# Attention's second product on 128 partitions instead of 99: probabilities padded with rows of zeros, values with rows of ones

## The chip, the cores and the metric

The kernel runs on one core of a Trainium2 chip. The metric is the device time of one execution in microseconds (us). Before the change it is 1243.13 us, the median of three runs (1242.87 to 1243.32).

Engines in the profile: PE is TensorE's matmul, PEld its weight load, DVE is VectorE, ACT is ScalarE, POOL is GpSimd, SP is the engine that issues most transfers. A matmul here has a stationary operand (loaded by a weight load, contraction rows x 128 columns) and a moving operand (the same contraction rows x N columns). N is called the width below, and the number of contraction rows is called the rows.

## The reference, cut to what matters

Two independent parts are put side by side along the last axis. Part A is a state-space layer. Part B, which the change touches, is attention over 64 segments of 32 tokens, each with 8 memory tokens, 32 heads of 128:

```python
for s in range(n_seg):                                   # 64 segments
    h = concat([mem, x[:, s*32:(s+1)*32]], axis=1)       # 40 rows
    q, k, v = h @ Wq, h @ Wk, h @ Wv                     # 32 heads of 128
    p = softmax(where(mask, q @ k.T * 128**-0.5, -1e9))
    o = (p @ v) @ Wo                                     # p @ v is the "second product"
    mem = o[:, :8]
    outs.append(o[:, 8:])
```

## The kernel before

It guesses the memory rows first, so that all segments can be worked on at once, and checks the guess at the end. Three segments and their three memory rows make one block of GW = 99 keys (96 tokens, GX = 96, and 3 memory rows). A unit is two heads by two blocks: four first products (k by q), one Exp on ACT, one masking product on POOL, and four second products. There are 16 head pairs x 11 units = 176 units, so 704 second products.

```python
# qk_init: buffers of the second product
for i in range(2):
    t = pool.tile([GW, NG, VW], BF16, name=f"b_v{i}", bufs=1)    # values: 99 partitions, 22 blocks, VW = 258
    G.memset(t[:, :, 0:1], 1.0)                                   # a column of ones gives the softmax sum
    G.memset(t[:, :, VW - 1:VW], 1.0)
for i in range(4):
    t = pool.tile([GW, 4 * GW + 32], BF16, name=f"b_m{i}", bufs=1)  # masked probabilities
    G.memset(t[:, 4 * GW:4 * GW + 32], 0.0)

def att_front(self, hp, u):
    for gg in range(2):
        g0 = (2 * u + gg) * GW
        for hh in range(2):
            j = 2 * gg + hh
            PE.matmul(s[:, j * GW:(j + 1) * GW], kt[:, hh, g0:g0 + 128], qt[:, hh, g0:g0 + GW], start=True, stop=True)
    # ... e = exp(s) on ACT ...
    k.G.tensor_tensor(v4(m[:, 0:4 * GW]), v4(e[:]), mask..., ALU.mult)   # POOL
    return m

def att_back(self, hp, u, m):
    for gg in range(2):
        for hh in range(2):
            j = 2 * gg + hh
            cs = slice(hh * 129, hh * 129 + 129)                  # 128 values and the ones column
            PE.matmul(o[:, gg, cs], m[:, j * GW:j * GW + 128], vt[:, 2 * u + gg, cs], start=True, stop=True)
    # ... reciprocal of the sums and normalisation on DVE ...

def attention(self):                                              # cut
    for n, (hp, u) in enumerate(units):
        pend.append((hp, u, self.att_front(hp, u)))
        if len(pend) > 2:
            self.att_back(*pend.pop(0))
        yield hp, u                                               # the projections of the next head pair go in between
```

So a unit is four matmuls of 99 columns on 128 rows, then four of 129 columns on 99 rows. What follows a unit has 128 rows again: a projection of 480 columns after 142 of the 176 units, and matmuls of 201, 512 or 73 columns after the other 34.

Of the kernel before, what the change touches and what calls it, by code (L numbers as in the profile page):

```python
# [9 lines left out]
BF16 = mybir.dt.bfloat16  # L10
I32 = mybir.dt.int32
ACT = mybir.ActivationFunctionType
ALU = mybir.AluOpType
# [17 lines left out]
NG = 22; GX = 96; GW = 99; NU = NG // 2  # L31
# [9 lines left out]
VW = 258  # L41
# [275 lines left out]
class PartB:  # L317
# [201 lines left out]
    def qk_init(self, pool):  # L519
        V, G = self.k.V, self.k.G  # L520
        self.qk = []
        for i in range(2):
            pair = []
            for n in "qk":
                t = pool.tile([128, 2, QW], BF16, name=f"b_{n}{i}", bufs=1)
                V.memset(t[:, :, 64 + NMX:GX], 0.0)
                V.memset(t[:, :, 21 * GW + 64:21 * GW + GX], 0.0)
                V.memset(t[:, :, NG * GW:QW], 0.0)
                pair.append(t)
            self.qk.append(pair)  # L530
        self.vmst = []
        for i in range(2):
            t = pool.tile([128, 4, 128], BF16, name=f"b_vmst{i}", bufs=1)
            V.memset(t[:, :, NM:128], 0.0)
            self.vmst.append(t)
        self.vb, self.mb = [], []
        for i in range(2):
            t = pool.tile([GW, NG, VW], BF16, name=f"b_v{i}", bufs=1)
            G.memset(t[:, :, 0:1], 1.0)
            G.memset(t[:, :, VW - 1:VW], 1.0)  # L540
            self.vb.append(t)
        for i in range(4):
            t = pool.tile([GW, 4 * GW + 32], BF16, name=f"b_m{i}", bufs=1)
            G.memset(t[:, 4 * GW:4 * GW + 32], 0.0)
            self.mb.append(t)

# [56 lines left out]
    def att_front(self, hp, u):  # L603
        k = self.k; PE = k.PE
        qt, kt = self.qk[hp % 2]
        s = k.ps("S")
# [5 lines that stand above are left out]
        e = self.p3.tile([GW, 4 * GW], BF16, name="b_e", bufs=3)  # L612
        i = hp * NU + u
        k.S.activation(e[:], s[0:GW, 0:4 * GW], ACT.Exp, scale=float(E) ** -0.5, accum_out=self.accE[0:GW, i:i + 1])  # L614
        m = self.mb[i % 4]
        mask = k.maskA if u == 0 else k.maskB
        v4 = lambda t: t.rearrange("p (a b q) -> p a b q", a=2, b=2)
        k.G.tensor_tensor(v4(m[:, 0:4 * GW]), v4(e[:]), mask[0:GW, :, :].unsqueeze(2).to_broadcast([GW, 2, 2, GW]), ALU.mult)  # L618
        return m

    def att_back(self, hp, u, m):
# [515 lines left out]
```

## Time and profile before

| what | number | where |
|---|---|---|
| span of the profiled run | 1240.8 us | head of the page |
| PE busy | 1234.9 us (100%) | busy table |
| PE waiting | 2.2 us, all in the first 16 us | list of waits |
| second product, first to last matmul | 502.0 to 1017.1 us | instructions of the values' tile |
| POOL idle before its first mask product | 31.15 us | timeline of POOL |

From the page of the kernel before: its head, two rows of its slices (PE, and the clock granted to it) and its chain by engine. In the slices each digit is for 1/40 of the span, in tenths:

```profile
span 1240.8 us, 19711 instructions
PE 1234.9 (100%) x8148; PEld 655.2 (53%) x8148; DVE 611.2 (49%) x1124; ACT 325.9 (26%) x754; POOL 199.9 (16%) x284
PE   9999999999999999999999999999999999999998
PEclk9999999999999999999999999999999999999999
PE 98%; DMA 1%; DVE 0%; issue 0%
```

The last of these lines is the chain of waits that ended last, by engine. PE is the limit from the first slice to the last, and the granted clock is 1.0 in the run's record. Apart from the 2.2 us of waits, nothing can shorten the run but a shorter matmul stream.

The list of waits of PE, before (who waited for whom, total us, times, longest us):

```profile
PE psO L913 <- PEq L1118: 0.9, 1, 0.9
PE psO L379 <- DMA a_hs<-in_B_x_dram: 0.6, 1, 0.6
PE psS L414 <- DVE b_xe L77: 0.5, 1, 0.5
PE psS L414 <- DMA a_hs<-in_B_Wv_dram: 0.2, 1, 0.2
```

The groups by shape, before (line, engine, operation, output<-inputs, output shape<-input shape, count, busy us, mean ns of one, idle before):

```profile
L629 PE MATMUL psO<-b_v,b_m 99*128 99x129 bf16 x704 | 70.4, 221 | 0.0
L611 PE MATMUL psS<-b_q,b_k 128*128 128x99 bf16 x704 | 60.1, 208 | 0.0
L629 PEld LDWEIGHTS <-b_m 99*128 99x128 bf16 x704 | 46.4, 99 | 0.5
L685 PEld LDWEIGHTS <-b_ol 128*128 128x128 bf16 x960 | 93.1, 98 | 109.3
```

The 221 ns of a second product is its latency; many overlap. What it costs the stream is the time from its start to the start of the next matmul, called its gap here. The weight load of 99 rows takes as long as one of 128.

The trace's records give each matmul's start to the nanosecond. Means by width, before (worked out from the starts):

```
what                          width  rows   gap, ns     width/2.4 + 2.5
output projection                512   128   215.9        215.8
projections                      480   128   202.5        202.5
last tile, third piece           128   128    55.8         55.8
guess                             64   128    29.1         29.2
projections of the memory        201   128    86.7         86.3
first product, 1st..4th of 4      99   128    44.5 44.9 44.0 45.3    43.8
second product, 1st..4th of 4    129    99    60.4 59.3 59.2 59.4    56.3
```

The formula in the last column is from the Trainium skill, "TensorE: Matmul & The Clock Gate", section "Back-to-back issue gap", which gives it for isolated matmuls. The multiples of 32 agree with it here to 0.1 ns, each matmul with its own weight load. The second product is over it by about 3 ns.

These are means over 176 units.

### The profile page before, as it was taken

The page shows a single profiled execution, that of the slowest core. Times are in us where ns is not written, and L with a number is a line of the kernel's source. Part 1 is how long each engine was busy: PE and PEld are TensorE (multiplying, and loading weights), DVE is VectorE, ACT ScalarE, POOL GpSimd, SP SyncE. Part 2 cuts the span into 40 slices and gives each one's busy share as a digit, 9 for nine tenths or more (in the row PEclk, how much of TensorE's full clock was granted, in tenths as well). Part 3 has the DMA queues.
Part 4 walks back from the last instruction along what each step waited for, and adds up shares of the span by engine and source line. Part 5 has one row for each costly group of instructions (what it writes and reads, how often), then busy time and mean ns, then how long its engine had stood idle before and what let it go on. Part 6 is the DMA issues. An engine that isn't in the chain of part 4 may idle for free.

```text
span 1240.8 us, 19711 instructions
## 1 busy us (share of the span) xinstructions
PE 1234.9 (100%) x8148; PEld 655.2 (53%) x8148; DVE 611.2 (49%) x1124; ACT 325.9 (26%) x754; POOL 199.9 (16%) x284
## 2 busy tenths in 40 slices
PE   9999999999999999999999999999999999999998
PEld 4444444444455445566666655655565554454444
DVE  4889999999941222444444444444444550011000
ACT  3344434444310001333333323333333230000000
POOL 2000000000032140222222222232222330000000
PEclk9999999999999999999999999999999999999999
DMA  9942232332566558577668554645575469607000
GB/s 223 260 130 68 85 94 68 102 94 77 153 189 202 158 161 170 100 151 150 138 122 173 123 136 95 129 77 103 106 139 106 72 203 231 140 18 153 17 18 28
DMA packets 306056, 153.95 MB, mean 124 GB/s; under 512 B 147242, under 2 KB 299810, under 8 KB 305962
## 3 DMA queue, kind: packets, MB, share of 16 engines
q1 hardware_dynamic: 304138, 150.82, 52.6%
q10 hardware_dynamic: 1824, 1.84, 0.5%
q8 instruction: 65, 1.06, 0.4%
q14 instruction: 29, 0.24, 0.1%
HBM read 73.70 MB, written 44.71 MB: 95 GB/s over the span
## 4 chain that ended last, share of the span: by engine, by line
PE 98%; DMA 1%; DVE 0%; issue 0%
PE psP L585 33%; PE psS L685 9%; PE psO L256 9%; PE psS L414 9%; PE psP L414 9%; PE psP L685 5%; PE psS L310 4%; PE psP L310 4%; PE psP L568 4%; PE psO L629 3%; PE psS L611 3%; PE psO L685 2%; PE psS L718 1%; PE psP L505 1%; PE psP L737 1%; PE psO L482 1%
## 5 line engine op out<-in xcount | busy, mean ns | idle before, releaser
L585 PE MATMUL psP<-b_xe,w 128*128 128x480 bf16 x2048 | 439.6, 366 | 0.0
L585 PEld LDWEIGHTS <-w 128*128 128x128 bf16 x2048 | 193.7, 98 | 183.5
L618 POOL TENSOR_TENSOR b_m<-b_e,maskB 99x396 bf16<-99x396 bf16 x160 | 139.4, 871 | 348.2 <-ACT b_e L614 348.2
L77 DVE CAST b_q<-psP 128x480 bf16<-128x480 f32 (+1 forms) x192 | 98.1, 532 | 145.4 <-PE psP L585 133.9
L414 PEld LDWEIGHTS <-b_xe 128*128 128x128 bf16 x1024 | 99.8, 98 | 121.3 <-DVE b_xe L77 1.1
L75 ACT ACTIVATE b_k<-psP 128x480 bf16<-128x480 f32 x128 | 73.1, 571 | 319.1 <-PE psP L585 319.1
L685 PEld LDWEIGHTS <-b_ol 128*128 128x128 bf16 x960 | 93.1, 98 | 109.3
L614 ACT ACTIVATE b_e<-psS 99x396 bf16<-99x396 f32 x176 | 87.4, 497 | 170.9 <-PE psS L611 165.5
L636 DVE TENSOR_TENSOR b_ot<-psO,b_rall 99x512 bf16<-99x512 f32 x176 | 121.7, 692 | 6.4
L256 PE MATMUL psO<-w,a_bt 128*128 128x512 bf16 x512 | 115.7, 379 | 0.0
L634 DVE RECIPROCAL b_rall<-psO 99x4 f32<-99x4 f32 x176 | 31.3, 178 | 132.8 <-PE psO L629 132.8
L685 PE MATMUL psS<-w,b_ol 128*128 128x512 bf16 x416 | 92.1, 379 | 0.0
L414 PE MATMUL psS<-w,b_xe 128*128 128x512 bf16 x384 | 90.7, 379 | 0.0
L414 PE MATMUL psP<-w,b_xe 128*128 128x512 bf16 x384 | 90.7, 379 | 0.0
L256 PEld LDWEIGHTS <-a_bt 128*128 128x128 bf16 x512 | 49.7, 98 | 59.0
L310 PEld LDWEIGHTS <-a_hs 128*128 128x128 bf16 x512 | 49.5, 98 | 58.3
L77 DVE CAST b_ost<-psS 128x512 bf16<-128x512 f32 x13 | 9.0, 692 | 125.4 <-PE psS L685 125.4
L629 PE MATMUL psO<-b_v,b_m 99*128 99x129 bf16 x704 | 70.4, 221 | 0.0
L611 PEld LDWEIGHTS <-b_k 128*128 128x128 bf16 x704 | 50.0, 98 | 33.9 <-DVE b_k L77 0.2
L611 PE MATMUL psS<-b_q,b_k 128*128 128x99 bf16 x704 | 60.1, 208 | 0.0
L75 ACT ACTIVATE b_vst<-psS 128x512 bf16<-128x512 f32 x56 | 33.4, 597 | 99.5 <-PE psS L414 75.6
L310 PE MATMUL psS<-w,a_hs 128*128 128x512 bf16 x256 | 57.9, 379 | 0.0
(203 smaller groups left out, 1097.9 us busy)
## 6 DMA issues: line engine op xcount, KB each, us to landing
b_v<-b_vx SPq DMA_DIRECT2D x16, 1056.0 KB
b_os<-b_ot SPq DMA_DIRECT2D x16, 960.0 KB
w<-in_B_Wv_dram SPq DMA_DIRECT2D x14, 1024.0 KB
b_vx<-b_vst SPq DMA_DIRECT2D x48, 256.0 KB
w<-in_B_Wo_dram SPq DMA_DIRECT2D x12, 1024.0 KB
w<-in_B_Wq_dram SPq DMA_DIRECT2D x16, 512.0 KB
w<-in_B_Wk_dram SPq DMA_DIRECT2D x16, 512.0 KB
a_xn<-in_A_x_dram SPq DMA_DIRECT2D x32, 128.0 KB
```

What stands on the lines that cost most here:

```text
L75: self.S.activation(out, in_, ACT.Copy)
L77: self.V.tensor_copy(out, in_)
L256: m = PE.matmul(u[:, i, :], self.bt[:, i, c, :], self.xT[tb][:, c, :], start=(c == 0), stop=(c == KC - 1))
L310: PE.matmul(py[:], self.hs[tb][:, pc, i, tt * 128:(tt + 1) * 128], self.ct[half, i][:, pc, :], start=(pc == 0 and i == 0), stop=(pc == PC ...
L414: m = self.k.PE.matmul(p[:], self.xe[:, c, t * 128:(t + 1) * 128], w[:, c, :], start=(c == 0), stop=(c == KC - 1))
L585: PE.matmul(p[:, 0:480], w[:, i * KC + c, hh * 128:(hh + 1) * 128], self.xe[:, c, 480 * q:480 * q + 480], start=(c == 0), stop=(c == KC - 1))
L611: PE.matmul(s[:, j * GW:(j + 1) * GW], kt[:, hh, g0:g0 + 128], qt[:, hh, g0:g0 + GW], start=True, stop=True)
L614: k.S.activation(e[:], s[0:GW, 0:4 * GW], ACT.Exp, scale=float(E) ** -0.5, accum_out=self.accE[0:GW, i:i + 1])
L618: k.G.tensor_tensor(v4(m[:, 0:4 * GW]), v4(e[:]), mask[0:GW, :, :].unsqueeze(2).to_broadcast([GW, 2, 2, GW]), ALU.mult)
L629: PE.matmul(o[:, gg, cs], m[:, j * GW:j * GW + 128], vt[:, 2 * u + gg, cs], start=True, stop=True)
L636: V.tensor_tensor(ot[:, 2 * u:2 * u + 2, :].rearrange("p g (h e) -> p g h e", h=2), oa[:, :, 1:257].rearrange("p g (h e) -> p g h e", h=2) ...
L685: k.PE.matmul(self.acc[t, half], ol[:, h8, tt * 128:(tt + 1) * 128], self.wo_half(half, h), start=(h == 0), stop=(h == H - 1))
```

## The change

Its intent is to let the second product contract over a full array of 128 rows. Rows 99 to 127 of the probabilities are zero and of the values one, so they add nothing. Exp, the mask product and the normalisation keep 99 partitions. (The mask's index is cut in the last line.)

```diff
-            t = pool.tile([GW, NG, VW], BF16, name=f"b_v{i}", bufs=1)
+            t = pool.tile([128, NG, VW], BF16, name=f"b_v{i}", bufs=1)
+            G.memset(t[GX:128, :, :], 1.0)
             G.memset(t[:, :, 0:1], 1.0)
             G.memset(t[:, :, VW - 1:VW], 1.0)
@@
-            t = pool.tile([GW, 4 * GW + 32], BF16, name=f"b_m{i}", bufs=1)
+            t = pool.tile([128, 4 * GW + 32], BF16, name=f"b_m{i}", bufs=1)
+            G.memset(t[GX:128, :], 0.0)
             G.memset(t[:, 4 * GW:4 * GW + 32], 0.0)
@@ att_front
-        k.G.tensor_tensor(v4(m[:, 0:4 * GW]), v4(e[:]), mask..., ALU.mult)
+        k.G.tensor_tensor(v4(m[0:GW, 0:4 * GW]), v4(e[:]), mask..., ALU.mult)
```

More of the change, by code (lines that the diff above doesn't have):

```diff
@@ L617, in att_front @@
         v4 = lambda t: t.rearrange("p (a b q) -> p a b q", a=2, b=2)
-        k.G.tensor_tensor(v4(m[:, 0:4 * GW]), v4(e[:]), mask[0:GW, :, :].unsqueeze(2).to_broadcast([GW, 2, 2, GW]), ALU.mult)
+        k.G.tensor_tensor(v4(m[0:GW, 0:4 * GW]), v4(e[:]), mask[0:GW, :, :].unsqueeze(2).to_broadcast([GW, 2, 2, GW]), ALU.mult)
         return m
```

## The prediction

> **What bounds the kernel.** TensorE, everywhere. The page's busy table gives PE 1234.9 of 1240.8 us (100%), the chain of waits is 98% PE, and the list of waits shows PE waiting 2.2 us in the whole run, all of it at the start. The granted clock is 1.0 throughout. So time moves only if the matmul stream becomes shorter or gets a hole.
>
> **What the change touches there.** The second attention product: 704 weight loads of b_m (99x128) and 704 matmuls of b_v (99 rows, 129 moving columns), all between 502 and 1017 us. Afterwards they have 128 rows. Nothing is removed and no column is added or taken away.
>
> From the groups by shape: the 99-row weight loads take 98 ns, as do all 128-row loads. The weight loads of both heights have the same four-chunk, 32-column read pattern, so the fast load is already on. The Trainium skill ("TensorE: Matmul & The Clock Gate", section on LDWEIGHTS) says that load time goes with columns, not rows; this trace agrees. The same page ("Back-to-back issue gap") gives N/2.4 + 2.5 ns from start to start. In the timeline of PE, 512 columns take 215.8 ns, 128 take 55.8, 64 take 29.1: exactly that. The second product takes 59.5 ns against 56.25 by the formula, also in the step to the next 128-row matmul (59.4). That is 3.2 ns over, and it doesn't vary with the head's or unit's alignment. Other odd widths with 128 rows are over by less: 73 by 0.8, 99 by 0.8, 201 by 0.4 ns.
>
> So the whole prize is about 3.2 ns x 704 = 2.3 us, 0.2%, if the partial rows cause that excess, and nothing if the odd width of 129 does. I give each about half. There is no larger row penalty hiding: no weight load here delays its matmul, since 64-column matmuls with their own loads run at 29 ns.
>
> **What it adds.** On POOL, at 465.8 us, two fills of 32 partitions x 5676 elements and four of 428. Existing fills took 108 ns for 25, 204 ns for 128 and 258 ns for 198 elements: about 0.85 ns an element, so an estimate of 4.9 us each for b_v and 0.4 us each for b_m, 11.5 us together. POOL is idle from 466.4 to 497.5 us there, and the DMA that first writes b_v is issued at 483.5 us. The fills should be done near 478 us: off the critical path. The per-unit mask product on POOL (871 ns), Exp, reciprocal and eviction keep 99 partitions. SBUF space per partition and DMA are unchanged.
>
> **Prediction.** 1242.0 us, range 1239.8 to 1244.3. Chances: faster by over 2% 0.01, within 2% 0.98, slower by over 2% 0.01.
>
> **What would show it.** Right: PE still busy for 100%; second product's rows 128; its weight loads still 98 ns; the gap from its start to the next start between 56.2 and 59.6 ns (56.2 means rows were the cause, 59.5 the width); POOL busy up by about 11 us, all before 480 us; b_v's DMAs at the same times. Wrong: a PE hole near 480 to 505 us, because the fills run slower than estimated and hold back the value loads or the first mask product.
>
> **What would make it wrong.** A reordering of the engines' programs by the changed dependencies (new holes in PE, some us); fills several times slower than estimated; a row-dependent cost in the first product's or projections' matmuls next to the second product that I can't see; a lower granted clock from the fuller array.

## The result, and the profile after

| | before | after |
|---|---|---|
| median of six runs, us | 1242.95 (1242.38 to 1243.32) | 1241.84 (1240.70 to 1242.67) |
| ratio | | 0.9991 (95%: 0.9978 to 1.0004) |
| second product, first to last matmul, us | 515.145 | 514.355 |

A ratio is the mean time of one kernel's fast runs over that of the other's in the same rounds, so it is not quite the ratio of the medians. The interval holds 1: the timing doesn't show that the change helps. The trace shows more. The stretch from the first to the last second product has no wait in it, and its length repeats to the nanosecond where the same matmuls run again (experiments 1 and 2 below), while the startup doesn't: the first projection matmul starts anywhere from 465.3 to 466.9 us in the profiled runs, with how late the first transfers land. So below this stretch, called the stage, is what small effects are read from.

The head of the page, its slices and its chain by engine, after:

```profile
span 1240.4 us, 19648 instructions
PE 1230.1 (99%) x8078; PEld 654.6 (53%) x8148; DVE 610.7 (49%) x1124; ACT 326.0 (26%) x754; POOL 211.6 (17%) x290
PE   8999999999999999999999999999999999999998
PEclk9999999999999999999999999999999999999999
PE 98%; DMA 1%; issue 0%; DVE 0%
```

The 99% and the 8 are no new waits: 8078 matmuls are on record against 8148 weight loads, so 70 records are missing, all but 3 of them outside the stage. POOL has 11.7 us more. The list of waits of PE, after:

```profile
PE psO L379 <- DMA a_hs<-in_B_x_dram: 0.9, 1, 0.9
PE psO L915 <- PEq L1120: 0.8, 1, 0.8
PE psS L414 <- DMA a_hs<-in_B_Wv_dram: 0.6, 1, 0.6
PE psS L414 <- DVE b_xe L77: 0.5, 1, 0.5
```

The waits are those of the startup, as before. The groups by shape, after (two lines moved down in the file, so L629 is L631 now, and L611 is L613):

```profile
L631 PE MATMUL psO<-b_v,b_m 128*128 128x129 bf16 x704 | 70.0, 221 | 0.0
L613 PE MATMUL psS<-b_q,b_k 128*128 128x99 bf16 x704 | 60.1, 208 | 0.1
L631 PEld LDWEIGHTS <-b_m 128*128 128x128 bf16 x704 | 46.0, 98 | 0.5
L687 PEld LDWEIGHTS <-b_ol 128*128 128x128 bf16 x960 | 93.1, 98 | 109.3
```

A second product on 128 rows takes 221 ns, as on 99. The timeline of POOL, after, around the new fills, and the first write of the values, issued by SP:

```profile
466.25 9.59 POOL L539 MEMSET b_v<- 32x5676 bf16 x2 [5.01 <-PE psP L310]
...
479.00 0.18 POOL L546 MEMSET b_m<- 128x32 bf16 x2
...
484.03 0.33 SPq L602 DMA_DIRECT2D b_v<-b_vx  x1
...
497.97 0.87 POOL L620 TENSOR_TENSOR b_m<-b_e,maskA 99x396 bf16<-99x396 bf16 x1 [18.79 <-ACT b_e L616]
```

The fills are over at 479.2 us, the values are written from 484.0 us on, and POOL still idles 18.79 us before its first mask product: the fills cost no time. PE agrees: from the first projection matmul to the first second product it takes 36.417 us before and after.

Gaps by place in the unit, worked out from the starts (ns; "projection" is the first 480-wide matmul after a unit):

```
                    second product, 1st..4th of 4    projection, 1st 2nd 3rd   stage, us
before              60.4  59.3  59.2  59.4           205.3 201.6 201.7         515.145
after               56.9  60.3  59.3  59.4           201.7 201.9 202.2         514.355
```

The projection's means are over the 142 units that one follows; expectation e2 below has 205.1 for the first. The change shortened two gaps of a unit: that of the first second product (60.4 to 56.9, with 1.0 given back at the next) and that of the first projection matmul after the unit (205.3 to 201.7, with 1.4 given back at the next three). Where 201-wide matmuls follow instead, in 14 units, the first of them does the same (89.7 to 85.7). All of these are matmuls whose row count, in the kernel before, differs from the one in front of them: 99 after 128, and 128 after 99. The third and fourth second products stand at 59.3 and 59.4 ns on 99 rows and on 128.

### The profile page after: what moved, and what is told of

Same layout as the page of the kernel before. It is cut to its first block, busy times and chain, and to the rows that moved or that the text cites. A ratio compares the mean times of both kernels' runs of the same rounds, so it can differ in the third digit from the quotient of the medians.

```text
span 1240.4 us, 19648 instructions
## 1 busy us (share of the span) xinstructions
PE 1230.1 (99%) x8078; PEld 654.6 (53%) x8148; DVE 610.7 (49%) x1124; ACT 326.0 (26%) x754; POOL 211.6 (17%) x290
## 4 chain that ended last, share of the span: by engine, by line
PE 98%; DMA 1%; issue 0%; DVE 0%
PE psP L587 33%; PE psS L687 9%; PE psO L256 9%; PE psS L414 9%; PE psP L414 9%; PE psP L687 5%; PE psP L310 4%; PE psS L310 4%; PE psP L570 4%; PE psO L631 3%; PE psS L613 3%; PE psO L687 2%; PE psS L720 1%; PE psP L505 1%; PE psP L739 1%; DMA a_hs<-in_B_Wv_dram 1%
## 5 line engine op out<-in xcount | busy, mean ns | idle before, releaser
L631 PE MATMUL psO<-b_v,b_m 128*128 128x129 bf16 x704 | 70.0, 221 | 0.0
L613 PEld LDWEIGHTS <-b_k 128*128 128x128 bf16 x704 | 50.0, 98 | 33.9 <-DVE b_k L77 0.2
L613 PE MATMUL psS<-b_q,b_k 128*128 128x99 bf16 x704 | 60.1, 208 | 0.1
```

## The experiments

**Theories.** S: a matmul whose row count differs from its predecessor's pays some 2 to 3 ns. Rival P, from the prediction: each of the 704 partial-row matmuls pays 3 ns. Rival N: the result was chance, or came from the fills. Apart from these: what holds the other gaps at 59.3 ns, as the rows don't; the prediction's other half was the odd width.

The first four ran together, in five rounds, on one chip.

### 1. The change again

> The changed kernel again, to see whether its 0.09% is there. Theory S (a switch of the row count between neighbouring weight loads costs about 2.5 ns, 352 switches, nothing else in the change matters): about 0.8 us less than before, ratio 0.9993 to 0.9995; first-to-last matmul of the second product 514.4 us against 515.15 before. Rival N (the first result was chance): ratio 1.000 and the stage back at 515.1. Rival P (each of the 704 partial-row matmuls pays about 3 ns, the prediction's guess): about 2.2 us, ratio 0.998.

Measured: 1241.99 us median against 1242.01 us before, ratio 0.9999 (0.9985 to 1.0013). The stage is 514.355 us, the same to the nanosecond as in the first run of the change. So the effect is real in the trace and too small for the timing: 0.79 us of 1242 is 0.06%, and the interval is 0.28% wide. P, which asked for about 2.2 us, does not fit the stage.

### 2. The fills alone

```diff
-                PE.matmul(o[:, gg, cs], m[:, j * GW:j * GW + 128], vt[:, 2 * u + gg, cs], start=True, stop=True)
+                PE.matmul(o[:, gg, cs], m[0:GW, j * GW:j * GW + 128], vt[0:GW, 2 * u + gg, cs], start=True, stop=True)
```

> The fills on POOL stay, the second product contracts over 99 rows again. If rows are the cause: time as before (ratio 1.000), the first of each unit's four gaps 60.4 ns again and the first projection gap after a unit 205.1 ns, stage 515.15 us. If the fills or the program's new layout were what moved it: stage 514.4 us and gaps as in the changed kernel.

Measured: 1242.74 us, ratio 1.0006 (0.9992 to 1.0019). Stage 515.145 us, again the same to the nanosecond as before; gaps 60.4 and 205.2 ns. The gain is the rows'. The fills lie before the stage, so it can't show their cost; but from the first projection matmul to the first second product PE takes 36.420 us with them here, against 36.417 without them in the kernel before. N falls.

### 3. 99 and 128 rows in turn

```diff
+                R = GW if j % 2 == 0 else 128
-                PE.matmul(o[:, gg, cs], m[:, j * GW:j * GW + 128], vt[:, 2 * u + gg, cs], start=True, stop=True)
+                PE.matmul(o[:, gg, cs], m[0:R, j * GW:j * GW + 128], vt[0:R, 2 * u + gg, cs], start=True, stop=True)
```

> Of a unit's four second products, the first and third contract over 99 rows, the second and fourth over 128: four switches of the row count a unit instead of two. Theory S: dearer than before, stage about 515.9 us (0.75 above before), and gaps of about 60 ns or more at every switch. Rival P (per partial matmul): between the two kernels, stage about 514.75 us.

Measured: 1242.30 us, ratio 1.0001 (0.9987 to 1.0014). Stage 514.764 us, where P had put it, and not the 515.9 us of S. But the gaps are not P's: 60.4, 59.2, 59.2, 59.4 ns, then 201.7 for the projection. The entry (99 after 128) pays as before, the exit is free because the last of the four now has 128 rows, and the two other 128-row matmuls are no faster for it. The switches within the four cost nothing that can be seen. So S as written was wrong in one point: a switch in front of a gap that already stands at 59.3 ns does not add to it.

### 4. An even width

The kernel before, with a pad column beside each column of ones: VW is 260, the slices are 130 wide, and the DVE reads shift by one column.

```diff
-VW = 258
+VW = 260
-                cs = slice(hh * 129, hh * 129 + 129)
+                cs = slice(hh * 130, hh * 130 + 130)
```

> The kernel before with its 99 rows, but 130 moving columns in place of 129 (a pad column next to the ones column). If an odd width is what keeps the gap at 59.3 ns: gaps near 56.7 ns (130/2.4 + 2.5), 2.6 ns x 528 or more, so stage about 513.5 us and 1.5 to 1.9 us less in all although one column more is streamed. If not the odd width but a width above 128: 59.3 ns or more, time as before or 0.3 us longer.

Measured: 1242.42 us, ratio 1.0004 (0.9991 to 1.0018). Gaps 60.4, 59.3, 59.2, 59.3 ns, stage 515.156 us. One column more changes nothing, and the odd width is not the cause. With experiment 2, both halves of the prediction's "rows or odd width" are now false for the middle gaps.

### 5 to 7. Where the blocks lie, and the width

Single runs on the changed kernel (128 rows), state unknown, read from the trace alone. In 5 the four blocks of b_m lie 128 columns apart instead of 99 (and b_m is zeroed whole). In 6 the second head's output starts at PSUM column 256 instead of 129. In 7 each of the 11 units of a head pair has another width. The DVE reads of the outputs move along in 6 and 7 (cut here).

```diff
 5
-                PE.matmul(o[:, gg, cs], m[:, j * GW:j * GW + 128], ...)
+                PE.matmul(o[:, gg, cs], m[:, j * 128:j * 128 + 128], ...)
 6
-                PE.matmul(o[:, gg, cs], ...)
+                PE.matmul(o[:, gg, hh * 256:hh * 256 + 129], ...)
 7
+                W = (129, 130, 131, 132, 136, 144, 160, 161, 192, 200, 256)[u]
+                a, z = (0, 0) if hh == 0 else (VW - W, 512 - W)
-                PE.matmul(o[:, gg, cs], m[:, j * GW:j * GW + 128], vt[:, 2 * u + gg, cs], ...)
+                PE.matmul(o[:, gg, z:z + W], m[:, j * GW:j * GW + 128], vt[:, 2 * u + gg, a:a + W], ...)
```

> The changed kernel with the four stationary blocks of b_m at column steps of 128 instead of 99, so each weight load starts at a multiple of 256 bytes. If the blocks' odd starts cause the 59.3 ns gaps: gaps 2 to 4 of a unit near 56.7 ns, stage about 513.0 us. If not: 59.3 ns, stage 514.36 us as in the changed kernel.

> The changed kernel with the second head's output at PSUM column 256 instead of 129. If where the outputs lie causes the 59.3 ns gaps: gaps after the second and fourth product (or all of gaps 2 to 4) near 56.7 ns, stage 513.0 to 513.7 us. If not: 59.3 ns, 514.36 us.

> The changed kernel, outputs spread over the bank, with another moving width in each of a head pair's 11 units: 129, 130, 131, 132, 136, 144, 160, 161, 192, 200, 256 (the columns beyond 129 are not used, the result stays right). A fixed surcharge of a second product would give width/2.4 + 5.1 ns at each width; a surcharge of narrow widths only would give 59.3 ns up to some width and width/2.4 + 2.5 beyond it; a floor of the weight load would give 59.3 ns up to 136 (136/2.4 + 2.5 is 59.2) and the formula from there.

Measured in 5: 56.9, 60.3, 59.2, 59.3 ns, stage 514.322 us. In 6: 56.9, 60.3, 59.3, 59.5 ns, stage 514.475 us. Neither place is the cause. In 7 (single time 1251.01 us, as more columns are streamed):

```
width   width/2.4 + 2.5   gaps, 1st..4th of 4, ns
 129        56.3          55.8  60.1  59.3  59.3
 130        56.7          56.6  60.9  59.1  59.2
 132        57.5          60.0  60.0  60.0  60.1
 136        59.2          58.3  62.5  61.8  60.3
 144        62.5          62.4  65.8  65.2  61.8
 160        69.2          69.2  69.0  73.4  68.4
 161        69.6          72.5  69.1  73.1  69.1
 192        82.5          81.6  81.7  86.7  81.9
 200        85.8          85.8  89.2  88.4  85.0
 256       109.2         109.3 109.2 113.3 108.3
```

None of the three written expectations holds at all widths. It is no floor of the weight load, since the surcharge stays above 136, and no fixed one, since 160, 192 and 256 are free of it in the second and fourth place. The third place pays 4 ns at these three too. The first of the four is at most 0.5 ns above the formula at every width but 132 and 161 (131, not shown, included), and what stands in front of it is a first product of 99 columns rather than another second product.

The scan ties each width to one unit, and the two exceptions belong to the unit: 132 is at unit 3 and 161 at unit 7, and in the changed kernel, with 129 columns everywhere, the first gap is 59.2 and 59.1 ns in just these two units and 55.6 to 56.8 ns in all others. So differences of 1 to 3 ns between two widths of this table may be the units'.

### 8. The first product on 99 rows too

The kernel before, with the first product cut to 99 of its 128 contraction rows; a single run, read from the trace. The scores are wrong; the scores of these inputs are so small that the output still passed the comparison.

```diff
-                PE.matmul(s[:, j * GW:(j + 1) * GW], kt[:, hh, g0:g0 + 128], qt[:, hh, g0:g0 + GW], start=True, stop=True)
+                PE.matmul(s[:, j * GW:(j + 1) * GW], kt[0:GW, hh, g0:g0 + 128], qt[0:GW, hh, g0:g0 + GW], start=True, stop=True)
```

> The kernel before, with the first product cut to 99 of its 128 contraction rows as well (scores wrong on purpose; the result may still be close, since the scores are tiny). Theory S' (what costs is the first matmul of another row count than its neighbour, not 99 rows as such): the second product's first gap falls from 60.4 to 56.9 ns as in the changed kernel, the surcharge moves to the first product's first gap (44.5 to about 47 or 48 ns), and the projection gap after a unit stays at 205 ns. If 99 rows as such cost in the first of four: the first gap stays at 60.4 ns.

Measured: the second product's gaps are 56.9, 60.3, 59.2, 59.3 ns, those of the changed kernel, although every one of them contracts over 99 rows. The surcharge went to the first product's first gap, 44.5 to 48.4 ns, and the projection after the unit stays at 205.2 ns. The stage is 515.058 us with two switches a unit, as many as before. So 99 rows are as fast as 128. What costs is the change from one count to the other.

### 9 and 10. The two products in turn

The eight matmuls of a unit are issued first, second, first, second, and so on, instead of four and four: once in the changed kernel (no switch of the row count anywhere), once in the kernel before (eight switches a unit). Apart from that and the change itself nothing differs.

```diff
-    def att_front(self, hp, u):
+    def att_front(self, hp, u, back=None):
@@ after each matmul of the first product
+                if back is not None:
+                    next(back, None)
@@ att_back, after each matmul of the second product
+                yield
@@ attention
-            pend.append((hp, u, self.att_front(hp, u)))
-            if len(pend) > 2:
-                self.att_back(*pend.pop(0))
+            back = self.att_back(*pend.pop(0)) if len(pend) > 1 else None
+            pend.append((hp, u, self.att_front(hp, u, back)))
+            for _ in back or ():
+                pass
```

> The changed kernel with the matmuls of the two products taken in turn (first, second, first, second ...), all on 128 rows. No row switch anywhere. It tells where the remaining 2.6 ns go: if they belong to a 129-column matmul that follows another one of 129, the second product's gaps fall to about 56.9 ns and the stage to about 513 us, with 1.3 us less than the changed kernel in all; if any matmul of an odd width pays when its neighbour is odd, nothing moves (514.4 us) or the first product's gaps rise instead.

> The kernel before with the same interleaving: 99-row and 128-row matmuls alternate, so a unit has eight switches of the row count instead of two. Theory S' (each first matmul of another row count pays about 2.5 to 3.9 ns): both products' gaps rise by 3 to 4 ns over those of the 128-row interleaving, 1400 switches, 3.5 to 5 us more than it, stage about 517 to 518 us, which a timing can resolve (ratio to before about 1.002). If the row count as such does not matter and the two switches were special to the ends of a group of four: stage within 1 us of the 128-row interleaving.

| | median of 5, us | ratio to before (95%) | stage, us | row switches in the stage |
|---|---|---|---|---|
| 9, on 128 rows | 1240.22 (1239.35 to 1240.64) | 0.9982 (0.9968 to 0.9995) | 513.205 | 0 |
| 10, on 99 rows | 1244.43 (1242.66 to 1245.09) | 1.0013 (0.9999 to 1.0027) | 516.444 | 1396 |

The kernel before has 1242.38 us in these rounds (9 runs). The 1396 switches count the two at the ends of the stage. Experiment 10 is less dear than the 3.5 to 5 us over experiment 9 that were expected: the stage has 3.24 us. By time the two differ by 4.21 us, and their runs don't overlap, while the interval of experiment 10 against the kernel before holds 1. The values' tile in the trace, for the kernel before, the changed one, experiment 9 and experiment 10 (count, least, median and longest ns of one, then first and last start in us):

```profile
L629 PE MATMUL psO<-b_v,b_m x704: 220/221/223, 502.0 to 1017.1; 99*128 99x129 bf16 x176
```

```profile
L631 PE MATMUL psO<-b_v,b_m x704: 218/221/223, 502.4 to 1016.7; 128*128 128x129 bf16 x176
```

```profile
L633 PE MATMUL psO<-b_v,b_m x704: 217/220/223, 501.6 to 1014.8; 128*128 128x129 bf16 x176
```

```profile
L631 PE MATMUL psO<-b_v,b_m x704: 220/221/223, 503.1 to 1019.5; 99*128 99x129 bf16 x176
```

Last start less first start is the stage, to 0.1 us: 515.1, 514.3, 513.2, 516.4. The latency of one matmul, 220 or 221 ns, doesn't betray any of it.

The timeline of PE around 700 us shows one unit each, experiment 9 first, then experiment 10 (start us, us, what):

```profile
700.13 0.21 PE L613 MATMUL psS<-b_q,b_k 128*128 128x99 bf16 x1
700.17 0.22 PE L633 MATMUL psO<-b_v,b_m 128*128 128x129 bf16 x1
...
700.53 2.94 PE L570 MATMUL psP<-b_xe,w 128*128 128x201 bf16 x32
```

```profile
700.76 0.21 PE L611 MATMUL psS<-b_q,b_k 128*128 128x99 bf16 x1
700.80 0.22 PE L631 MATMUL psO<-b_v,b_m 99*128 99x129 bf16 x1
...
701.18 1.78 PE L585 MATMUL psP<-b_xe,w 128*128 128x480 bf16 x8
```

From the unit's first matmul to the projection's: 0.40 us on one row count, 0.42 us with a switch at each. Means from the starts:

```
              first product, 1st..4th    second product, 1st..4th
9,  128 rows  44.5  45.3  44.5  44.7     56.8  56.3  57.1  56.7
10, 99 rows   44.4  47.2  46.6  46.8     60.3  59.4  59.3  59.5
```

Two things follow. First, experiment 9 has few gaps of 59 ns left: 88 of 703, against 559 in the changed kernel, nearly all of the 88 in units 3, 7 and 9. Its second products run at 56.7 ns on average, the formula's value for 130 columns. So in this kernel a 129-column matmul pays some 2.6 ns when it follows another one of its kind, and in most units not when it follows the 99-column product. Second, the 1396 switches of experiment 10 cost 516.444 - 513.205 = 3.24 us, or 2.3 ns each. The 352 switches of the kernel before against none after are 0.79 us, or 2.2 ns each. Experiment 8 against the changed kernel has 352 switches for 0.70 us, 2.0 ns each. Quite different counts give nearly the same price, except that the switches within the four of experiment 3 were free. The second product's gaps in experiment 10 are those of the kernel before to 0.1 ns, 59.3 to 60.3 ns: a switch and a neighbour of its own kind each bring such a gap to about 59.3 ns, and the two together not further.

Experiment 9 is the fastest kernel: its ratio to before excludes 1, and its stage is 1.94 us shorter than before and 1.15 us shorter than with the change alone.

## Why the prediction was right or wrong

The predicted 1242.0 us against a measured 1241.84 us is right in the total, and most of its steps held; the step that sized the gain did not.

- **PE is the only limit, and nothing but the matmul stream counts: right.** All PE waits are in the startup, before and after.
- **No large row penalty; the weight load takes the same time at any height: right.** 99 rows 99 ns, 128 rows 98 ns in the means. The Trainium skill says so ("TensorE: Matmul & The Clock Gate", section "LDWEIGHTS"), and its table "Why this matters for your kernels" says the same of the matmul: on 32 rows alone it takes the time of one on 128. This agrees for 99 and 128: 59.3 ns in the third place for both, and experiment 8's second products on 99 rows match the changed kernel's on 128 to 0.1 ns.
- **The fills, 11.5 us on POOL, done near 478 us, off the critical path: right.** 9.6 + 1.8 us measured, done at 479.2 us. The stretch of PE that they lie beside keeps its length to 3 ns (experiment 2).
- **"The whole prize is about 3.2 ns x 704 = 2.3 us, 0.2%, if the partial rows cause that excess, and nothing if the odd width of 129 does": wrong.** Neither is the cause. What the rows cost is 2.2 ns per switch, at 352 switches: 0.79 us. Most of the rest of the excess belongs to second products that follow one another (experiment 9), and an even width leaves it in place (experiment 4). The predicted 1.1 us gain, the middle of two false alternatives, came near the 0.79 us of the stage by luck.
- **"Also in the step to the next 128-row matmul (59.4)": misread.** The cost of leaving the 99 rows does not sit in that gap, but in the next one, the first projection's: 205.3 ns against 201.7 ns for its neighbours. It was in the trace of before, hidden in a mean of 202.5 ns. The prediction's list of dangers had named a row-dependent cost in the projections beside the second product as a thing it could not see.
- **"... it doesn't vary with the head's or unit's alignment": wrong for the units.** The first gap is 59.1 or 59.2 ns in units 0, 4 and 8 and 60.8 or 60.9 ns in the others, in the trace of before. The total did not rest on it.
- **The 1.1 us between the two medians is not shown to be the change's.** The repeat gave 0.02 us. Only the stage's 0.79 us is.

Left open: why a second product that follows another one pays 2.6 ns. It is not its rows, an odd width, or where the weight blocks or outputs lie. Where the moving operands lie was not tested, though it changes from unit to unit and the gaps do too; the pattern of every fourth unit stays in experiment 4, where the values' blocks lie further apart. In the width scan the surcharge is absent in the second and fourth place at 160, 192 and 256 columns and present in both at 130 and 136. Why a row switch does not add to it (experiment 3) is open too. Only 99 rows against 128 were tried, and the weight load and its matmul always changed together, so which of the two pays is not shown.

## What to carry to other kernels

Here, with TensorE saturated, padding a contraction from 99 to 128 rows made no matmul faster by itself. It helped only where neighbours in the stream then had the same row count, at some 2 ns per switch, and not where the gap stood at 59.3 ns already. When an effect is smaller than the spread of the times, look for a stretch of the trace without waits and measure its length; and split mean gaps by their place in the sequence, and by unit, as a mean over all of them hid half of this effect. The order in which short matmuls of two kinds are issued can be worth more than their shapes: in the stage, taking the two products in turn gained 1.15 us on top of the change's 0.79 us, without moving any work.

## What the Trainium skill lacked or had wrong

- "TensorE: Matmul & The Clock Gate", "Back-to-back issue gap": it gives about 81 ns for each matmul of 128 columns and 131 ns for 512 columns in a real stream of weight loads and matmuls. Here, with a weight load for each matmul, the gaps are 55.8 and 215.9 ns, which is the formula that the section calls the isolated one.
- The same section: the formula fits multiples of 32 (64, 128, 480, 512) to 0.1 ns here, but 129 columns one after another take 59.3 ns instead of 56.3, and 99 columns 44.0 to 45.3 in the means (43.2 to 47.7 by unit) instead of 43.8.
- No page that I read has a cost for a change of the row count between neighbouring matmuls: 2.2 ns each over 352 switches, 2.3 ns each over 1396.
- The same page, "LDWEIGHTS": columns/1.2 would be 107 ns for 128 columns; the records show 98 ns, and 64-column matmuls with their own loads follow at 29.1 ns. The section doesn't say how its figure goes with the fast weight load that the page describes further down.
- "GPSIMD Engine Reference" names memset and gives no rate for it by name: 5676 bf16 elements on 32 partitions took 4822 ns, 0.85 ns an element.
